# A new order of the matmuls, a later booking for one unit's values, and query loads joined into one

## The chip, the cores and the metric

The kernel runs on one core of a Trainium2 chip. The metric is the device time of one execution, in microseconds (us). A core has a matrix engine (TensorE, PE in the profile, with its weight loads as PEld), VectorE (DVE), ScalarE (ACT), GpSimd (POOL) and SyncE (SP), which in this kernel issues all DMAs.

## The reference

Two branches work on the same input `x` of 2048 rows of 512, and a gate per row mixes them. Branch A is attention with 32 heads of 16 columns that share one key and one value head; branch B is a gated feed-forward layer with 1792 inner columns. All is float32.

```python
q = (x @ wq).reshape(B, S, 32, 16)           # 32 query heads
k, v = x @ wk, x @ wv                        # one head of 16 columns each
p = softmax(einsum("bhqd,bkd->bhqk", q, k) * 16 ** -0.5)
a = einsum("bhqk,bkd->bhqd", p, v).reshape(B, S, 512) @ wo
b = (sigmoid(x @ w_gate) * (x @ w_up)) @ w_down
g = sigmoid((x * gate_w).sum(-1, keepdims=True))
return g * a + (1 - g) * b
```

## The kernel before

**The work.** The 2048 rows fall into four blocks of 512, and the heads into eight groups of four: 32 units of attention. Float32 operands of the projections are split into a high and a low part, so that one product becomes three matmuls. For a unit, line L1136 multiplies queries with keys to find each row's maximum (a "max" matmul, whose bank VectorE reduces on L1138), and L1145 multiplies again, the other way round and with the maximum taken off (a "score" matmul, whose bank ScalarE turns into exponentials `p` on L1147). Line L1009 multiplies `p` with the values (a "values" step of eight matmuls over all 128 rows of the array, here called V). Line L1110 is the feed-forward layer and the output projection (a "fill" matmul). Max, score and fill matmuls use one half of the array's rows, 64, and two of them run side by side, one in each half.

**The order is written out by hand.** `ORDER` is a string with one character for each step of TensorE. A hexadecimal digit is a slot: its two upper bits tell what the upper half does and its two lower bits what the lower half does (0 nothing, 1 max, 2 score, 3 fill). `V` is a values step, `G` a group of the first projections (L854) or a turn of the values (L926), and `.` no instruction at all, only a planned wait. V and G use the whole array, slots its halves; a run of V is opened after a slot and closed by the next slot. `plan()` walks the string with a model of all engines (class `State`), in which a slot is 100 units long. The model decides which of the eight PSUM banks each matmul takes (the one that has been free longest, `take`), and where each instruction of the other engines and each DMA stands in its engine's queue. The engines then run these queues in order, each waiting for what it needs. No time of the model is enforced on the chip. A booking in the model only keeps a string from being accepted in which a step comes too early: a bank that DVE has read counts as free `FREE` units after the read, one that ACT has read `FREE_A` units after it.

**Runs of V.** All V of a run add into one bank, taken when the run opens (`issue_v`), and when the run closes ACT copies that bank out (`finish`, L1016); if the unit has earlier runs, POOL adds the copy to theirs (L1023). So the bank that a run opens on must have been read out, by DVE if its last user was a max matmul (L1136), by ACT if it was a score matmul (L1145).

**Queries.** `store_q` writes the high and low part of a projected block of queries to DRAM (L955). `load_q` fetches a unit's queries into one of three tiles `qs` (L969): for each half of the array high, high and low part, 16 rows each, six DMAs of 64 KB; from the fourth unit on two DMAs of zeros follow (L971). The model books a load as six issues, in the changed kernel too. Unit u+1 is loaded when the max matmuls of unit u begin; the first two units are loaded together at the start.

**The end of a unit.** `store` sends the unit's sums and outputs to DRAM; `sums` fetches the sums (L1037) and the outputs `vd` (L1039); DVE inverts the sums (`invert`); `send_inverse` writes them back (L1047); `spread` fetches them spread over rows (`bc`, L1053); POOL multiplies the two (`divide`, L1058). Two units share a tile of 128 rows. Unit 30, the last but one (`NU - 2`), fills both halves of its own, so its fetches come twice; its result feeds the last fill matmuls (the `e` jobs). Unit 31 is finished in the tail, after the last V.

**Second halves of a fill job.** A fill job's two halves swap banks in the middle, and a marker on SP's queue (L1114) hands over: if SP is held up, that fill waits.

Of the kernel before, what the change touches and what calls it, by code (L numbers as in the profile page):

```python
# [9 lines left out]
F32 = mybir.dt.float32  # L10
# [7 lines left out]
S, D, H, DH, F = 2048, 512, 32, 16, 1792  # L18
# [34 lines left out]
IN, OUT, VALUES = 52, 106, 371  # L53
# [69 lines left out]
class State:  # L123
# [170 lines left out]
    def event(self, what, args):  # L294
# [374 lines left out]
    "GGGGGGG555G55G555G55......5G55GG555G55G555GG55G555GG5dddGff7f77ffffd757d.GG7fffdfffd7f7ffffdedee7edef7ef7b7b7b7b"  # L669
    "bdfedebdfbdb79ffef55VVVV7b76bfdbf9fbdef9fe7ededee7f6f7bdef6fdff7775VVV9deedef7edf9fbe77bfb7bb7bdff9edb7fedfd75dV"  # L670
    "VVVVGV6fede.edfef7efbb7f9fb7b7b7bfed9fbdb7fedbfed7d5VV655VVV7b7bb7fededbf9e7fbdededeef77b7ef9faf7d7f7ddVVVV5bb77"
    "bbbffde79fefededeede7bf77bfbd6fff7ddd5VVV566VV6ddefe7eedf6fbfe7b7b7b7bbdfbdfededbb7fedbf5VV555VVV97b7fbdbdbfb7eb"
    "fdedededeef76ffb76fef9f6fbf5V5a6V996VV696V559VVV7b7b7bbfdbdbedfe7edeeddee7fb7fed6feedf7777bVVVV9deeedf7fedb7bdef"
    "b7b7bb77eefddeedfef9b7ffdbddfedd5VVVVV6e9ff77bfb7b7bb77bfedbbdf6ff9f9ff.dd66VV659VV659VV7b7b7bbdfedbedfe79feedde"
    "e7f6f7bf9fbf6f6ffd5VVVVV7b97b7bbfdf9fee7efdedeede77efdbe7fee7feedfbdbfed9dVVVVV56fbfe7bfb7b7bb77bfbdafdbdf7bfedf"
    "de.56VV65aV6a5V955VVV97bbb77ffbdbdee7fededeede7f7b7bbfdbf9fbfb7e7aff775VVVV9dedfbdee7fedeeddef6fe7e7e7bfdbff775."
    "5VVVVV9deff9f6fbd6fedefb7b7b7bbdff9f9bf7ef97edefaV65eVVV959VV677bbfdfeeddee7f6ff797VVVdede7efb7b7b7bedbdff9eVVVd"
    "edede7ef6f6fbf97bfb7bb7bdff9f6efdbf6dbeff615.VVVVV6deededf7bf6feb7fbdb7bb7bbdfdfbdb7ef6edf5fdVVVVV5edeef7bfe7ede"
    "7e7bfb7b7bbdff9dbf6f9fedbf6fdV5a6V9aaVVVVV6dedef7ef6f6fbdbfb7e727b7bdef9fdbfbdef9f6f6f.9VV955VVV6edff6defb7ed6fb"
    "fe7b7bb7bdedfedfb7bf97edbfd4.9VV656VV5a5VV97bfdbdbe7f6fedefe7e763b7befdedefdbdefb7b79f.5VVV9a5V595VVV7b7afdedbf7"  # L680
    "b79fefbdedeedee77ff6f9fe7edb7bf7V95aV669V99aVV695VVV7b7afdf97efedef6fedb7b7bbdff96ffbd6fbffddd5VVVV677bbb7fdbfed"
    "bf6fededeede77fbfba7fdbf7fddd5VVVV767bbb7bffdedbe7fedededee7fb7f6ef7edbfd7f79VVVVV97bbb77fdef9f6fedefbde4ee7defe"
    "7dbf9fbb7f9ff55.VVVVVV7b79bffa7fdebdb7fededeedef7f6fe7e7bf9f9f6f7VVV969VV6edeedf7fb79fee7f9fb7b7bb7bfdedfbdef9f6"
    "ffd545.VVVVV96edffb7bf7edb7bbfdedeede7ef7defe7ebdb7bbf9VVVVV5baV9b7b7bb7fdfe7bedfedededee7ff6f67bfbdbfd7fd5VVVVV"
    "5edeeedfb7f6fe7bef7bb7b7bfddeefdbdbfa7f7eebV996V965VV5a9VV6a5VV6dedef7bfb79fbf9fb7edeede7ef7e7efdef97b7ffedefedd"
    "9VVVVV69f7bff6fb7b7bb7b7f9fedebdbf79ffefe5.6VV955VVV9b7b7fdbfb79fee7fededeede7ef7deef7ef67bffd9ffdedd5VVVVV67b7f"
    "bf9b7fe7b7bb7fededeedf7bbbd7ff5.5VVVVVdedede6ff6fb7bdb7efb7bb7bdef7edfedbf97bfed715.VV59aVVVV7b7bb5fee7fbdebdfbd"
# [564 lines left out]
```

## Time and profile before

| | us |
|---|---|
| median of 3 runs | 1583.15 |
| lowest and highest of them | 1582.33 and 1583.36 |
| the profiled execution | 1581.56 |
| its span, first to last instruction | 1579.8 |
| PE, DVE, ACT, POOL busy in it | 1570.6, 1335.6, 1223.0, 785.7 |

The profiled execution is 1.59 us faster than the median, and 1.76 us of its time lie outside the span. A busy engine is not an engine without waits: matmuls overlap, one record lasts 0.39 us while slots follow each other faster, so a wait shorter than the overlap leaves no idle time in PE's row. It is seen in the distance between the starts of two slots. The idle time of PEld, the weight loads, is not lost time by itself, since a weight load is short and runs beside the matmul before it.

### The profile page before, as it was taken

To read this page: it belongs to the slowest core of one execution; us is meant where nothing else is said; L and a number is where in the kernel's file an instruction comes from. 1 tells how busy PE (TensorE), PEld (TensorE's weight loads), DVE (VectorE), ACT (ScalarE), POOL (GpSimd) and SP (SyncE) were. 2 spreads that over 40 slices of the span, in tenths; PEclk is the share of its full clock that TensorE was granted. 3 is DMA by queue.
4 is the path that set the end of the run, shared out by engine and by line. 5 is a ranking of instruction groups with operands and counts; after the bars stand their busy time and mean duration, and the time that the engine had idled before them with its cause. 6 is when DMAs were issued, how large, how long until landed. Compare 5 with 4: busy or idle time off the path is not lost.

```text
span 1579.8 us, 33611 instructions
## 1 busy us (share of the span) xinstructions
PE 1570.6 (99%) x12910; PEld 1018.7 (64%) x12910; DVE 1335.6 (85%) x2280; ACT 1223.0 (77%) x2415; POOL 785.7 (50%) x713
## 2 busy tenths in 40 slices
PE   9999999999999999999999999999999999999998
PEld 7776766666666665756665666666666667676663
DVE  7998998988798888889889878897978899898852
ACT  4276778878788778868788877877878888787897
POOL 4226463745574164367466236265657426537351
PEclk9999999999999999999999999999999999999999
DMA  7413120212122121122121212022212212111011
GB/s 254 154 55 91 45 62 30 66 53 89 42 80 61 48 80 52 33 73 73 47 82 53 76 36 85 16 66 67 75 42 89 66 34 79 53 36 56 16 56 48
DMA packets 63077, 103.44 MB, mean 65 GB/s; under 512 B 24530, under 2 KB 24786, under 8 KB 62916
## 3 DMA queue, kind: packets, MB, share of 16 engines
q1 hardware_dynamic: 62916, 101.29, 20.5%
q8 instruction: 102, 1.67, 0.4%
q14 instruction: 59, 0.48, 0.1%
HBM read 79.51 MB, written 21.75 MB: 64 GB/s over the span
## 4 chain that ended last, share of the span: by engine, by line
PE 98%; DVE 1%; DMA 0%; POOL 0%; issue 0%; ACT 0%; DVEq 0%; SPq 0%; ACTq 0%
PE bank L1110 32%; PE bank L1009 29%; PE bank L1136 17%; PE bank L1145 16%; PE bank L854 3%; DVE mx L1138 1%; PE bank L1191 0%; DMA wkv_raw<-wkv 0%; POOL wkv_s L757 0%; PE bank L926 0%; DVE q L949 0%; DVE wkv_stack L890 0%; DVE ba L1200 0%; DVEq L1248 0%; ACT ou_last L1173 0%
## 5 line engine op out<-in xcount | busy, mean ns | idle before, releaser
L1138 DVE TENSOR_REDUCE mx<-bank 128x1 f32<-128x512 f32 x2048 | 1249.7, 680 | 172.9 <-PE bank L1136 85.9
L1147 ACT ACTIVATE p<-bank 128x512 f32<-128x512 f32 x2048 | 1037.2, 661 | 4.5 <-PE bank L1145 1.4
L1145 PE MATMUL bank<-qs,ks 64*128 64x512 f32 x2048 | 721.6, 401 | 0.0
L1136 PE MATMUL bank<-ks,qs 64*128 64x512 f32 x2048 | 680.7, 407 | 0.0
L1009 PE MATMUL bank<-p,v_aug 128*32 128x512 f32 x4096 | 477.5, 597 | 0.0
L1136 PEld LDWEIGHTS bank<-ks,qs 64*128 64x128 f32 x2048 | 337.5, 184 | 133.2 <-issue 49.7
L1145 PEld LDWEIGHTS bank<-qs,ks 64*128 64x128 f32 x2048 | 358.7, 184 | 89.5 <-ACT p L1147 20.1
L1016 ACT COPY ou<-bank 128x512 f32<-128x512 f32 x194 | 117.0, 603 | 281.1 <-PE bank L1009 196.0
L1023 POOL TENSOR_TENSOR ou<-ou,ou 128x512 f32<-128x512 f32 x163 | 210.0, 1288 | 210.9 <-ACT ou L1016 207.8
L1110 PE MATMUL bank<-wd,hl 64*128 64x512 f32 x1344 | 278.3, 391 | 0.1
L1110 PE MATMUL bank<-x,wu 64*128 64x512 f32 x1344 | 278.0, 391 | 0.1
L1009 PEld LDWEIGHTS bank<-p,v_aug 128*32 128x32 f32 x4096 | 114.7, 109 | 253.5 <-issue 208.5
L1110 PE MATMUL bank<-x,wg 64*128 64x512 f32 x1344 | 275.2, 391 | 0.0
L1110 PEld LDWEIGHTS bank<-wd,hl 64*128 64x128 f32 x1344 | 204.0, 184 | 19.7 <-issue 4.2
L1110 PEld LDWEIGHTS bank<-x,wu 64*128 64x128 f32 x1344 | 203.5, 185 | 14.8 <-issue 1.7
L1110 PEld LDWEIGHTS bank<-x,wg 64*128 64x128 f32 x1344 | 201.8, 185 | 16.1 <-issue 2.0
L1089 POOL TENSOR_TENSOR ba<-ba,pa_d 128x512 f32<-128x512 f32 x31 | 39.6, 1284 | 102.8 <-ACT pa_d L1086 102.8
L830 POOL CAST wg<-rg 128x1024 fp32r<-128x1024 f32 x27 | 28.0, 1038 | 123.5 <-PE bank L1110 66.2
L757 POOL TENSOR_TENSOR wd<-rd,wd 128x512 fp32r<-128x512 f32 x56 | 72.3, 1291 | 4.5
L757 POOL TENSOR_TENSOR hl<-h,hl 128x512 fp32r<-128x512 f32 x56 | 71.9, 1284 | 4.5
L1110 PE MATMUL bank<-wa,o 64*128 64x512 f32 x360 | 71.4, 393 | 0.0
L830 POOL CAST wu<-ru 128x1024 fp32r<-128x1024 f32 x27 | 28.0, 1038 | 82.1 <-PE bank L1110 65.0
(82 smaller groups left out, 745.1 us busy)
## 6 DMA issues: line engine op xcount, KB each, us to landing
rg<-wg SPq DMA_DIRECT2D x28, 512.0 KB
ru<-wu SPq DMA_DIRECT2D x28, 512.0 KB
rd<-wd SPq DMA_DIRECT2D x28, 512.0 KB
qs<-qd SPq DMA_DIRECT2D x192, 64.0 KB
qd<-q SPq DMA_DIRECT2D x32, 256.0 KB
od<-ou SPq DMA_DIRECT2D x31, 256.0 KB
xf<-x_in SPq DMA_DIRECT2D x16, 256.0 KB
vd<-od SPq DMA_DIRECT2D x32, 128.0 KB
```

Source lines behind the costliest of these rows:

```text
L757: lo.tensor_tensor(hl[:, 1, :], raw, f32(hl[:, 0, :]), op=ALU.subtract)
L830: nc.gpsimd.tensor_copy(WS[item][:, 0, :], raw)
L854: nc.tensor.matmul(ps, w[:, p, part(kc)], X[b, kc][:, q, :], start=i == 0, stop=i == 3 * KC - 1)
L1009: nc.tensor.matmul(ps[32 * j:32 * j + 32, :], v_aug[:, c, :], PT.pop((u, c, j)), start=start, stop=stop)
L1016: nc.scalar.copy(to, ps)
L1023: nc.gpsimd.tensor_tensor(SUMS[u], SUMS[u], PARTS_OF[u].pop(0), op=ALU.add)
L1089: nc.gpsimd.tensor_tensor(BA[b, t], BA[b, t], PA[b, t].pop(0), op=ALU.add)
L1110: ins = nc.tensor.matmul(banks[i], l, r, start=start, stop=stop)
L1136: nc.tensor.matmul(banks[i], qs_t[u % 3][r, pr, part(qt)], ks[r, kb * 512:(kb + 1) * 512], start=True, stop=True)
L1138: nc.vector.tensor_reduce(MX[u][:, pr, h, qt, kb:kb + 1], banks[i], axis=AX.X, op=ALU.max)
L1145: nc.tensor.matmul(banks[i], ks[r, part(c)], qs_t[u % 3][r, pr, :], start=True, stop=True)
L1147: nc.scalar.activation(p, banks[i], AF.Exp, scale=0.25)
```

## The change

The string `ORDER` is replaced. The new one has 4251 slots for 4263 (26 slots with an idle half become 2, and the matmuls stay the same), 512 V as before, in 197 runs for 182, 24 G in 12 groups for 11, and 19 planned waits for 43. The model's `FREE` goes from 30 to 65 units and `FREE_A` from 55 to 62, and some durations, in hundredths of a slot, are raised by about half a per cent.

`store_q` writes the high part twice, so that DRAM holds the three parts in the order of the tile, and `load_q` fetches a half with one DMA of 48 rows (192 KB) in the place of three. Its source has the parts as its outermost dimension. For unit 30 `sums` no longer fetches the outputs; `spread` does, each half behind that half's inverses, and `divide` is booked 2300 units later.

```diff
-LATE, LATE_A, FREE, FREE_A = 188, 196, 30, 55
+LATE, LATE_A, FREE, FREE_A = 188, 196, 65, 62
...
-RED, GATED, SUM, ENDS, INVERSE, LOWER = 258, 258, 285, 115, 70, 285
+RED, GATED, SUM, ENDS, INVERSE, LOWER = 260, 258, 285, 115, 70, 285
...
+SPREAD_TWICE = 2300
-EXP, COPY, SCALED = 208, 210, 247
+EXP, COPY, SCALED = 209, 211, 250
...
-IN, OUT, VALUES = 52, 106, 371
+IN, OUT, VALUES = 52, 109, 373
...
             if u % 2 or u == NU - 2:
-                self.task(2, at + 2 * SAFE, "divide", u)
+                self.task(2, at + 2 * SAFE + (u == NU - 2) * SPREAD_TWICE, "divide", u)
...
-    "GGGGGGG555G55G555G55......5G55GG555G55G555GG55G555GG5dddGff7f77ffffd757d.GG7fffdfffd7f7ffffdedee7edef7ef7b7b7b7b"
+    "GGGGG.GG555G55G555G55.......5G55GG555GG555GG7757G57fddfffffffdd..ddfffffffffd7775GG555GG555G55Ga7bfdfbdb7efbdb7f"
...
-        qd = dp.tile([2, 2, 2, DH, 2, TB], F32, name=f"qd{b}_{t}")
-        for i, half in enumerate(QD[b, t]):
+        qd = dp.tile([3, 2, 2, DH, 2, TB], F32, name=f"qd{b}_{t}")
+        for i, half in enumerate((QD[b, t][0], *QD[b, t])):
             nc.sync.dma_start(qd[i].rearrange("g par d pr t -> (g par d pr) t"), f32(half))
...
         for par in range(2):
-            for n, i in enumerate((0, 0, 1)):
-                r = 64 * par + n * DH
-                nc.sync.dma_start(qs[r:r + DH], qd[i, g % 2, par].rearrange("d pr t -> d (pr t)"))
+            r = 64 * par
+            nc.sync.dma_start(qs[r:r + 3 * DH], qd[:, g % 2, par].rearrange("n d pr t -> n d (pr t)"))
             if u > 2:
-                nc.sync.dma_start(qs[64 * par + 62:64 * par + 64], zeros)
+                nc.sync.dma_start(qs[r + 62:r + 64], zeros)
...
-        for r in (0, 64) if u == NU - 2 else (64 * (u % 2),):
+        if u == NU - 2:
+            VD["last"] = od
+        else:
+            r = 64 * (u % 2)
             nc.sync.dma_start(VD[u // 2][0][r:r + 64, :], od.rearrange("(j r) t -> j r t", j=4)[:, :DH, :])
...
         for r in (0, 64) if u == NU - 2 else (64 * (u % 2),):
             nc.sync.dma_start(VD[u // 2][1][r:r + 64, :], sums.unsqueeze(1).to_broadcast([4, DH, TB]))
+            if u == NU - 2:
+                nc.sync.dma_start(VD[u // 2][0][r:r + 64, :],
+                                  VD["last"].rearrange("(j r) t -> j r t", j=4)[:, :DH, :])
```

How the rows move on TensorE shows at the run of V that opens with step 2 of unit 5. A row has its line, the bank it writes, and its operands (`ks` keys, `qs` queries, `x`, `wu` and the like fill operands, `p` exponentials). Before, TensorE's queue there reads:

```order
L1145 MATMUL bank_79<-qs_109,ks 128x512
L1009 MATMUL bank_74<-p_1_0_0_4153,v_aug 32x512
L1009 MATMUL bank_74<-p_1_0_1_4071,v_aug 32x512
L1009 MATMUL bank_74<-p_1_1_0_4136,v_aug 32x512
L1009 MATMUL bank_74<-p_1_1_1_4064,v_aug 32x512
L1136 MATMUL bank_78<-ks,qs_107 128x512
L1145 MATMUL bank_72<-qs_109,ks 128x512
L1136 MATMUL bank_75<-ks,qs_108 128x512
L1136 MATMUL bank_73<-ks,qs_108 128x512
L1110 MATMUL bank_77<-x_1_125,wu_6_3965 128x512
L1145 MATMUL bank_76<-qs_109,ks 128x512
L1009 MATMUL bank_79<-p_2_0_0_4201,v_aug 32x512
```

The last row opens the run on bank_79, which a score matmul (L1145) wrote last, so an exponential on ACT has to have read it. In the changed kernel, whose max, score, fill and values lines are L1141, L1150, L1115 and L1008, TensorE's queue at the same step reads:

```order
L1141 MATMUL bank_76<-ks,qs_107 128x512
L1115 MATMUL bank_72<-x_1_125,wu_6_4002 128x512
L1115 MATMUL bank_75<-x_1_125,wu_6_4002 128x512
L1115 MATMUL bank_72<-x_1_125,wu_6_4002 128x512
L1141 MATMUL bank_78<-ks,qs_107 128x512
L1141 MATMUL bank_73<-ks,qs_107 128x512
L1115 MATMUL bank_75<-x_1_125,wu_6_4002 128x512
L1141 MATMUL bank_79<-ks,qs_107 128x512
L1115 MATMUL bank_75<-x_1_125,wu_6_4002 128x512
L1115 MATMUL bank_72<-x_1_125,wu_6_4002 128x512
L1141 MATMUL bank_74<-ks,qs_107 128x512
L1008 MATMUL bank_76<-p_2_0_0_4138,v_aug 32x512
```

The run now opens on bank_76, which a max matmul wrote and DVE has read. Counted over the whole queue, the runs of V before open 83 times on a bank last written by a max matmul, 66 times by a score matmul, 25 times by a fill and 8 times by an earlier V; in the changed kernel 144, 29, 17 and 7 times.

Of SP's DMAs at the start (`qd` the stored queries in DRAM, `qs` the units' query tiles, 107 for unit 0 and 108 for unit 1) its queue before holds:

```order
L955 DMA qd_0_204<-q_0_0_188 128x512
L955 DMA qd_0_204<-q_0_1_189 128x512
L955 DMA qd_1_236<-q_1_0_220 128x512
L955 DMA qd_1_236<-q_1_1_221 128x512
L969 DMA qs_107<-qd_0_204 16x1024 x6
L969 DMA qs_108<-qd_0_204 16x1024 x6
```

and in the changed kernel:

```order
L955 DMA qd_0_204<-q_0_0_188 128x512 x2
L955 DMA qd_0_204<-q_0_1_189 128x512
L955 DMA qd_1_237<-q_1_0_221 128x512 x2
L955 DMA qd_1_237<-q_1_1_222 128x512
L968 DMA qs_107<-qd_0_204 48x1x1024 x2
L968 DMA qs_108<-qd_0_204 48x1x1024 x2
```

The twelve loads of the first two units have become four, of three times the rows, and each store of a query block has a third DMA. Of SP's DMAs at unit 30 (`sd`, `od`, `rd` in DRAM) its queue before holds:

```order
L1031 DMA sd_20017<-ou_19455 4x512
L1032 DMA od_20018<-ou_19455 128x512
L1037 DMA rc_20066<-sd_20017 128x16
L1039 DMA vd_20015<-od_20018 64x1x512 x2
L1047 DMA rd_20109<-rc_20066 128x16
L1053 DMA bc_20016<-rd_20109 64x1x512 x2
```

and in the changed kernel:

```order
L1030 DMA sd_19940<-ou_19453 4x512
L1031 DMA od_19941<-ou_19453 128x512
L1036 DMA rc_19986<-sd_19940 128x16
L1049 DMA rd_20033<-rc_19986 128x16
L1055 DMA bc_19939<-rd_20033 64x1x512
L1057 DMA vd_19938<-od_19941 64x1x512
L1055 DMA bc_19939<-rd_20033 64x1x512
L1057 DMA vd_19938<-od_19941 64x1x512
```

The inverses no longer stand behind the two fetches of `vd`; these come between and behind the spread inverses.

More of the change, by code (lines that the diff above doesn't have):

```diff
@@ L674 @@
[L674 to L683, printed above, removed]
@@ new lines @@
+    "edeeded7bfe7be7def6ffb7f5.5VVVV9dedef7bfe7eb7defbdb7b7bbfde7fed9fb7fffdd55VVVV67b7bfdefe7bf9f6bfdededeef7f6efde7"
+    "efb7bb7f9VV555VVV9deededffb7bf67ee7f777bbbffedfedb7bdff7dd5VVVVV9b7efddefe76fedbfbdb7bb7b7fedbdf9fef6f6ff5dVVVVV"
+    "dedeeddefe7eb77bb7fb7b7bbfddefed6fbdef7f775VVVVdedededefb7b7be7bdfb7b7bbfddbbdfb7ef6edfef5VV955VVV977efbdbfe7bb7"
+    "f9fededdeee7fe77bfb7ede7eff79V955VVVVV7b7bb7b7fbdbededdefededeef7b7bf7edbfedbfbe6V555VVV7b7bb77bbfd6fedefededeed"
+    "dfbe7f6fedbbb7fdf75VV969V5a5VV569VV696V97bbfdbdfb7af7deef7edeede7f7edbfb7bf9f6ffd5VV565VVVdedaf7bf7ebdf6fedfb7b7"
@@ new lines @@
+    "bbdbdf9fef6f6fbdffd56VV565VVV5edeefdbf6fafd7bfbdb7bb7bfdf6efdedb7bbfdef5VV656VVV5ededeeff6fbe7bdfb7b7bb7bdfbdf9f"
+    "b7bdefedfe5V555VVVVV67bdfe7efedbed7efbdb7bb7bdfedfe7edee7bffb7aV955VVVV7b7bbddef9fb7e7bdefededee7fb7fedb7bde7eff"
+    "9bVVVVVV7b7b7bb7bdfeedf9fededeede7f7b7efb7efadfd77dVVVVV7b7bbfdedeededf6fbbfa7V95aV655VVdedeef7b7b7bb7fedbdf5dVV"
+    "7b7bb7f9fededee7fb7deeedef7f6bdfe7edbfbfb57VVVVV5edefee7fed9fe7bfb7b7bb7bfdedefd6febdbf7bf5VV956VVVde5edeeffe79f"
+    "eb7bf77bbb7bfdf9fedef97bf6ffd9V659VV695VVV97b7bf7bfedebd7bfededdeeef7f6fe7bdbb7ef7efaV955VVVVV5b7bfbdbf9f6fbedef"
@@ L713 @@
+    "aVV6edff6f9fbdef67b7fe9fbVVV6dfbf6bdfb7afdbdf6fbeeV5a9VVV7b7b7bb7fbdbdedefedededeef77b7bfb7bedfefeeaVVaaaVVVaaaV"
+    "VVeffbbffaffafaeVVbfbffbfbfeeeea8VVaaaVVaaaVVbfbefffbfbeeeeVbfeefefbffbbaVaaaVVVaaaVVeefbfffbaVV.....V"
 )
```

63 lines of the change are left out of this document (30 added, 33 removed).

## The prediction

> **What bounds the kernel now.** I read the page first, for busy shares and the chain of work that ended last, then TensorE's timeline for the distance between starts, then the list of waits, and last SP's timeline with the DMA table by stretches.
>
> ```profile
> PE 1570.6 (99%) x12910; PEld 1018.7 (64%) x12910; DVE 1335.6 (85%) x2280; ACT 1223.0 (77%) x2415; POOL 785.7 (50%) x713
> ...
> PE 98%; DVE 1%; DMA 0%; POOL 0%; issue 0%; ACT 0%; DVEq 0%; SPq 0%; ACTq 0%
> ```
>
> TensorE carries 98% of the chain. So the time is the number of its steps by what each costs, plus its waits, and other engines count only where TensorE waits for them. The price of a slot stands in its timeline (start, duration, engine, line):
>
> ```profile
> 600.04 0.39 PE L1145 MATMUL bank<-qs,ks 64*128 64x512 f32 x1
> ...
> 600.26 0.39 PE L1136 MATMUL bank<-ks,qs 64*128 64x512 f32 x1
> ...
> 600.50 0.39 PE L1145 MATMUL bank<-qs,ks 64*128 64x512 f32 x1
> ...
> 600.73 0.39 PE L1136 MATMUL bank<-ks,qs 64*128 64x512 f32 x1
> ...
> 601.42 0.42 PE L1145 MATMUL bank<-qs,ks 64*128 64x512 f32 x1
> ...
> 601.69 0.38 PE L1145 MATMUL bank<-qs,ks 64*128 64x512 f32 x1
> ```
>
> Three slots from 600.04 to 600.73 are 0.69 us, so a slot is 0.23 us. The pair at 601.42 is 0.27 apart: a wait of 0.04 that no idle time shows. Runs of V look so:
>
> ```profile
> 1541.56 0.40 PE L1145 MATMUL bank<-qs,ks 64*128 64x512 f32 x2
> 1541.90 1.92 PE L1009 MATMUL bank<-p,v_aug 128*32 128x512 f32 x16
> 1543.75 0.96 PE L1145 MATMUL bank<-qs,ks 64*128 64x512 f32 x6
> 1544.64 0.64 PE L1009 MATMUL bank<-p,v_aug 128*32 128x512 f32 x4
> ```
> ```profile
> 425.94 0.43 PE L1145 MATMUL bank<-qs,ks 64*128 64x512 f32 x1
> 426.05 0.39 PE L1136 MATMUL bank<-ks,qs 64*128 64x512 f32 x1
> 426.38 1.92 PE L1009 MATMUL bank<-p,v_aug 128*32 128x512 f32 x16
> ...
> 429.12 2.78 PE L1009 MATMUL bank<-p,v_aug 128*32 128x512 f32 x24
> 431.83 0.49 PE L1136 MATMUL bank<-ks,qs 64*128 64x512 f32 x1
> ```
>
> A run of two V lasts 1.85 us (1541.90 to 1543.75) and one of three 2.71 (429.12 to 431.83), so a V is 0.86. From opening to opening, 1541.90 to 1544.64, two V and three slots take 2.74; less 2 x 0.86 and 3 x 0.23 that leaves 0.33 for going into the whole array and out again. The opening itself is 0.34 after the last slot at 1541.56, but 0.44 at 425.94. The second one waits 0.10. Its bank was last written by a score matmul, nine matmuls earlier. Who ends such waits (waiter, releaser, total us, times, longest; PEld is the weight load in front of the matmul):
>
> ```profile
> PEld bank L1136 <- ACT p L1147: 23.8, 54, 0.8
> ...
> PEld bank L1136 <- DVE mx L1138: 22.7, 41, 0.8
> PEld bank L1009 <- ACT p L1147: 22.4, 71, 0.9
> PEld bank L1145 <- ACT p L1147: 20.1, 45, 0.8
> ...
> PEld bank L1145 <- DVE mx L1138: 14.9, 51, 0.8
> ...
> PEld bank L1009 <- DVE mx L1138: 10.8, 33, 0.4
> ```
>
> V's weight load (L1009) is released 71 times by an exponential and 33 times by a maximum, though more runs open on a bank from a max matmul (83) than from a score matmul (66). The totals are idle time of the loader, an upper bound on what TensorE lost.
>
> **The change, part by part.** *Slots.* Pairing the half-empty ones saves 12 slots by 0.23: -2.8 us.
>
> *Switches.* 15 more runs of V and one more group of G, 16 by 0.33: +5.3. Each new run also makes a copy and an addition:
>
> ```profile
> L1023 POOL TENSOR_TENSOR ou<-ou,ou 128x512 f32<-128x512 f32 x163 | 210.0, 1288 | 210.9 <-ACT ou L1016 207.8
> ...
> L1016 ACT COPY ou<-bank 128x512 f32<-128x512 f32 x194 | 117.0, 603 | 281.1 <-PE bank L1009 196.0
> ```
>
> 15 by 0.60 on ACT and by 1.29 on POOL lie in the 23% and 50% that these engines idle: nothing, at most 9 us if ACT were the bound.
>
> *Openings.* 37 fewer runs open on a bank that ACT has to free (66 to 29). At the 0.10 of the row at 425.94 this is -3.7. The ends are 0, if the bank isn't the cause, and -12.6, if all loader idle counted (22.4 by 37/66). I take the price nearest to the term, the one measured at an opening.
>
> *Slots' own waits.* `FREE` grows by 35 units, 0.08 us at 0.23 a slot, which exceeds the wait of 0.04 at 601.69. The two rows with DVE hold 92 waits; at 0.04 they are 3.7 us. `FREE_A` grows by 7 units, 0.02 us, so the 99 waits for ACT mostly stay. I take half of 3.7, -1.8, since fuller slots ask for banks more densely; the ends are 0 and -7.6 (all 191). The planned waits, 43 to 19, issue nothing and are not counted again.
>
> *SP's queue.* A unit's load drops from six issues to two, so markers of fill jobs wait less behind it:
>
> ```profile
> L1110 PEld LDWEIGHTS bank<-wd,hl 64*128 64x128 f32 x1344 | 204.0, 184 | 19.7 <-issue 4.2 <-ACT pa_d L1086 0.8 <-SPq L1114 0.8
> L1110 PEld LDWEIGHTS bank<-x,wu 64*128 64x128 f32 x1344 | 203.5, 185 | 14.8 <-issue 1.7 <-SPq L1114 0.4 <-DVE mx L1138 0.2
> ```
>
> TensorE lost at most 1.2 us to them; I take -0.5.
>
> *The joined load.* Its source has three parts as outermost dimension. The nearest rows are those of `vd` and `bc`, whose source has four. First SP, POOL and TensorE at unit 30, then two stretches with the share of the 16 DMA engines and GB/s at the end; in the first of them only the two `vd` loads run:
>
> ```profile
> 1552.01 1.07 SPq L1053 DMA_DIRECT2D bc<-rd  x2
> ...
> 1557.30 1.30 POOL L1058 TENSOR_TENSOR vd<-vd,bc 128x512 f32<-128x512 f32 x1 [16.50 <-DMA bc<-rd]
> ...
> 1564.70 0.50 PE L1110 MATMUL bank<-we,o 64*128 64x512 f32 x1
> ```
> ```profile
> 1546.50:1548.50 2.00, 2.00 (x22) 1.00 (x22) 0.00 (x0) 2.00 (x5) 0.00 (x0) 1.00 0.26 100
> ...
> 30.00:40.00 10.00, 9.90 (x47) 6.64 (x45) 9.64 (x17) 5.46 (x11) 7.30 (x6) 1.00 1.04 369
> ```
>
> A share of 0.26 is four engines, 25 GB/s each, where other transfers reach 369 on sixteen. So I estimate three engines and 75 GB/s for the new load: 192 KB in 2.6 us, both halves in 5.2. Two `bc` of 128 KB took 5.29 us from issue to POOL, 2.6 of it for the bytes, so some 2.7 come on top. Later a load is issued when the max matmuls of the unit before begin, up to a unit's time ahead (1579.8 / 32 = 49 us), which hides 8 us; if that cover were gone, each of 30 loads would cost up to 8. At the start there is no such cover:
>
> ```profile
> 18.21 6.39 SPq L969 DMA_DIRECT2D qs<-qd  x12
> ...
> 20.61 3.02 PE L854 MATMUL bank<-x,wkv_s 128*128 128x512 f32 x12
> 23.56 1.30 PE L1136 MATMUL bank<-ks,qs 64*128 64x512 f32 x6
> ```
>
> The first max matmul runs at 23.56 without a gap. With both halves there at 18.21 + 5.2 + 2.7 = 26.1 it would wait 2.5. I take +2.0, as part of the 2.7 is the second issue, which overlaps. The ends are 0 (the twelve small loads were in time) and +7.7, below. The third store of each block is issued while SP waits for the next block.
>
> *Unit 30.* Its divide began at 1557.30 and its fills only at 1564.70, so nothing waits. The inverses lose the two `vd` loads in front of them, and these come behind instead: the divide starts about when it did. Zero; the cover is some 4 us after the divide's own 3.4.
>
> The sum is -2.8 + 5.3 - 3.7 - 1.8 - 0.5 + 2.0 = -1.5 us. Against the profiled execution, 1581.56, this is 1580.1; the median of the runs lies 1.6 higher, so 1581.6.
>
> **The rivals.** *The margins clear most waits.* Openings -6 (the fill banks too, and longer waits than 0.10), slots -5, the start +1.0: -2.8 + 5.3 - 6 - 5 - 0.5 + 1 = -8.0, 1575.1. For it speaks that the loader's waits add up to over 100 us; against it, that the one slot wait I can price is 0.04.
>
> *An opening costs what it costs.* If the wait comes from draining the halves before the whole array is used, the bank doesn't matter, the openings' term is 0 and the sum +2.2, 1585.4. Against it: openings at 1541.90 and 426.38 follow the same kind of slot and differ by 0.10. The Trainium skill, "TensorEngine Tiling (Array Packing)", section Tiling Modes, states such a drain at every change of tiling mode.
>
> *The joined load costs nothing.* If it spreads over sixteen engines after all, it lands before 23.56, as two issues take less of SP than six: the sum without the +2.0 is -3.5, 1579.6. Against it: the stretch at 1546.50, where a load with an outermost four moves 100 GB/s. The Trainium skill, "DMA: Bandwidth & Descriptors", section Bandwidth, says to batch DMAs, and that transfers under 64 KB are dominated by descriptors; by that page the joined load can only gain.
>
> *The first loads are served in turns* (slower). If three engines serve the loads of units 0 and 1 side by side, unit 0 is complete only with all four: 18.21 + 10.4 + 2.7 = 31.3, a wait of 7.7 in the place of 2.0. The sum is +4.2, 1587.4. It decides from a wait of 6.7 on. Against it: the small loads of one queue were issued, and used, one after another.
>
> **How the numbers follow.** The forecast has a chance of 0.32, the cleared waits 0.28, the free load 0.10, the fixed opening cost 0.12, the loads in turns 0.18. A measurement tells about 0.2%, 3.2 us, from no change. The forecast and the fixed opening lie within it: 0.44 same; the cleared waits and the free load 0.38 faster; the loads in turns 0.18 slower. The range goes from 1574.5, just below the cleared waits, to 1588, just above the loads in turns.
>
> **What would show it.** TensorE's first max matmul at some 25.5 us in place of 23.56 with a DMA as releaser; fewer waits of L1008's weight load ended by ACT, about 30 for 71; fewer slot waits ended by DVE; the same 0.33 at a clean switch; and the fills of unit 30 without a wait. The forecast is wrong if the new order waits for something that the old one never met, such as POOL behind a weight load that is itself queued behind a three-engine query load.

## The result and the profile after

| | before | after |
|---|---|---|
| median, us | 1582.91 (6 runs, 1581.33 to 1583.82) | 1587.76 (6 runs, 1587.41 to 1591.08) |
| profiled execution, us | 1581.56 | 1591.08 |
| its span, us | 1579.8 | 1589.3 |

The changed kernel is slower: the ratio is 1.0036, with a 95% interval of 1.0025 to 1.0046, and the medians lie 4.85 us apart. The profiled execution of the changed kernel lies 3.3 us above its median; some 2.1 of that is a slow first stretch, shown at the end.

The page's first line and the chain of work that ended last, after:

```profile
PE 1572.6 (99%) x12910; PEld 1016.0 (64%) x12910; DVE 1340.6 (84%) x2279; ACT 1230.4 (77%) x2429; POOL 804.5 (51%) x727
...
PE 96%; DMA 1%; DVE 1%; ACT 0%; POOL 0%; issue 0%; SPq 0%; DVEq 0%; POOLq 0%; ACTq 0%
PE bank L1115 32%; PE bank L1008 29%; PE bank L1141 16%; PE bank L1150 16%; PE bank L854 2%; DMA qs<-qd 1%; DMA md<-sq 1%; DVE mx L1143 0%; POOL wg L831 0%; DVE q L949 0%; DMA qs<-md 0%; ACT x L781 0%; PE bank L1196 0%; DMA wkv_raw<-wkv 0%;
```

TensorE carries 96% of the chain in place of 98%, and two transfers have come onto it: the query load, and `md`, by which the maxima are put into place for the scores. In order of time the chain has them here (start, us, what):

```profile
21.27 8.87 DMA qs<-qd
31.83 4.32 PE bank L854 x12
...
84.36 8.45 DMA md<-sq
```

And TensorE's timeline at both places:

```profile
23.73 2.00 PE L854 MATMUL bank<-x,wkv_s 128*128 128x512 f32 x8
26.47 0.50 PE L1141 MATMUL bank<-ks,qs 64*128 64x512 f32 x1 [0.74 <-DMA qs<-qd]
30.18 1.65 PE L1141 MATMUL bank<-ks,qs 64*128 64x512 f32 x5 [3.22 <-DMA qs<-qd]
31.76 4.39 PE L854 MATMUL bank<-x,wq 128*128 128x512 f32 x12
...
95.13 0.47 PE L1150 MATMUL bank<-qs,ks 64*128 64x512 f32 x1 [3.18 <-DMA qs<-md]
```

The first max matmul waits 0.74 us for the first half of unit 0's queries, the second 3.22 us for the other half, and the first score matmul 3.18 us for the maxima. The twelve query matmuls at 31.76 take 4.3 us; twelve like them took 3.0 us before. The reason stands in the column of the granted clock. The same execution by stretches (stretch, length, busy time of PE, PEld, DVE, ACT and POOL, granted clock, DMA share, GB/s):

```profile
29.00:30.00 1.00, 0.00 (x0) 0.00 (x0) 0.00 (x0) 0.00 (x0) 0.00 (x0) 0.50 0.22 74
30.00:35.00 5.00, 4.82 (x13) 3.45 (x14) 3.08 (x5) 0.00 (x0) 0.00 (x0) 0.53 0.46 146
96.00:99.00 3.00, 3.00 (x16) 2.75 (x18) 1.38 (x2) 1.56 (x4) 0.00 (x0) 0.52 1.03 384
```

From 28 to 35 us, and from 96 to 99, TensorE has half its clock: each wait is followed by a stretch of slow work. The first row has every other engine idle and a DMA share of 0.22 at 74 GB/s, near the 0.19 of three engines in sixteen; by this share the joined load runs on three. The Trainium skill, "DMA: Bandwidth & Descriptors", section Rules for kernel authors, says that an outermost dimension of fewer than 16 confines a DMA to at most that many engines; the source here has 3, and the trace agrees.

SP's timeline, and below it who ended SP's waits between 20 and 40 us:

```profile
20.38 3.02 SPq L968 DMA_DIRECT2D qs<-qd  x4
...
25.09 12.47 SPq L766 DMA_DIRECT2D xf<-x_in  x8
...
80.53 1.47 SPq L968 DMA_DIRECT2D qs<-qd  x2
...
84.36 0.40 SPq L993 DMA_DIRECT2D md<-sq  x1
...
92.86 1.39 SPq L1001 DMA_DIRECT2D qs<-md  x2
```
```profile
SPq L766 <- DMA qs<-qd: 9.1, 4, 3.4
```

Before, SP's timeline had:

```profile
25.59 3.81 SPq L766 DMA_DIRECT2D xf<-x_in  x8
```

SP took 12.47 us to issue eight loads of the next rows of `x`, where it had taken 3.81: for 9.1 us it was held until a joined load was done.

Elsewhere the new order did what was forecast. Who ended the waits of TensorE's loader, after:

```profile
PEld bank L1150 <- ACT p L1152: 36.5, 76, 0.8
PEld bank L1141 <- ACT p L1152: 33.0, 65, 0.8
PEld bank L1008 <- ACT p L1152: 10.8, 31, 0.6
PEld bank L1141 <- DVE mx L1143: 10.3, 17, 0.8
PEld bank L1008 <- DVE mx L1143: 8.9, 29, 0.4
...
PEld bank L1150 <- DVE mx L1143: 2.8, 5, 0.8
```

V's waits ended by an exponential fell from 71 to 31, and the slots' waits ended by a maximum from 92 to 22 (17 and 5). The slots' waits ended by an exponential rose from 99 to 141 (76 and 65). Averaged over all openings, the distance from the last slot's first matmul to the first V fell from 0.380 us to 0.359; what that distance holds is taken up under the openings.

### The profile page after: what moved, and what is told of

Same layout as the page of the kernel before. It is cut to its first block, busy times and chain, and to the rows that moved or that the text cites. A ratio compares the mean times of both kernels' runs of the same rounds, so it can differ in the third digit from the quotient of the medians.

```text
span 1589.3 us, 33458 instructions
## 1 busy us (share of the span) xinstructions
PE 1572.6 (99%) x12910; PEld 1016.0 (64%) x12910; DVE 1340.6 (84%) x2279; ACT 1230.4 (77%) x2429; POOL 804.5 (51%) x727
## 4 chain that ended last, share of the span: by engine, by line
PE 96%; DMA 1%; DVE 1%; ACT 0%; POOL 0%; issue 0%; SPq 0%; DVEq 0%; POOLq 0%; ACTq 0%
PE bank L1115 32%; PE bank L1008 29%; PE bank L1141 16%; PE bank L1150 16%; PE bank L854 2%; DMA qs<-qd 1%; DMA md<-sq 1%; DVE mx L1143 0%; POOL wg L831 0%; DVE q L949 0%; DMA qs<-md 0%; ACT x L781 0%; PE bank L1196 0%; DMA wkv_raw<-wkv 0%; DVE x L787 0%
## 5 line engine op out<-in xcount | busy, mean ns | idle before, releaser
L1150 PE MATMUL bank<-qs,ks 64*128 64x512 f32 x2048 | 726.0, 399 | 3.5 <-DMA qs<-md 3.5
L1141 PE MATMUL bank<-ks,qs 64*128 64x512 f32 x2048 | 678.0, 406 | 4.0 <-DMA qs<-qd 4.0
L1008 PE MATMUL bank<-p,v_aug 128*32 128x512 f32 x4096 | 480.9, 597 | 0.0
L1150 PEld LDWEIGHTS bank<-qs,ks 64*128 64x128 f32 x2048 | 360.0, 184 | 104.9 <-ACT p L1152 36.5
L1141 PEld LDWEIGHTS bank<-ks,qs 64*128 64x128 f32 x2048 | 337.8, 184 | 133.9 <-issue 50.6
L1015 ACT COPY ou<-bank 128x512 f32<-128x512 f32 x207 | 127.8, 617 | 277.9 <-PE bank L1008 133.4
L1022 POOL TENSOR_TENSOR ou<-ou,ou 128x512 f32<-128x512 f32 x176 | 227.0, 1290 | 175.4 <-ACT ou L1015 171.7
L1115 PE MATMUL bank<-x,wu 64*128 64x512 f32 x1344 | 274.2, 392 | 0.1
L1115 PE MATMUL bank<-wd,hl 64*128 64x512 f32 x1344 | 273.2, 390 | 0.0
L1115 PE MATMUL bank<-x,wg 64*128 64x512 f32 x1344 | 271.8, 391 | 0.0
L1008 PEld LDWEIGHTS bank<-p,v_aug 128*32 128x32 f32 x4096 | 113.2, 109 | 247.3 <-issue 219.4
L1115 PEld LDWEIGHTS bank<-x,wu 64*128 64x128 f32 x1344 | 204.4, 185 | 18.0 <-issue 2.5
L1115 PEld LDWEIGHTS bank<-wd,hl 64*128 64x128 f32 x1344 | 203.8, 184 | 17.2 <-issue 3.4
L1115 PEld LDWEIGHTS bank<-x,wg 64*128 64x128 f32 x1344 | 201.1, 184 | 16.9 <-issue 2.5
L1115 PE MATMUL bank<-wa,o 64*128 64x512 f32 x360 | 69.9, 391 | 0.2 <-SPq L1119 0.2
```

Of the source, the lines that this page charges most:

```text
L1008: nc.tensor.matmul(ps[32 * j:32 * j + 32, :], v_aug[:, c, :], PT.pop((u, c, j)), start=start, stop=stop)
L1015: nc.scalar.copy(to, ps)
L1022: nc.gpsimd.tensor_tensor(SUMS[u], SUMS[u], PARTS_OF[u].pop(0), op=ALU.add)
L1115: ins = nc.tensor.matmul(banks[i], l, r, start=start, stop=stop)
L1141: nc.tensor.matmul(banks[i], qs_t[u % 3][r, pr, part(qt)], ks[r, kb * 512:(kb + 1) * 512], start=True, stop=True)
L1150: nc.tensor.matmul(banks[i], ks[r, part(c)], qs_t[u % 3][r, pr, :], start=True, stop=True)
```

## The experiments

My theory was that the loss is the three-engine load with what follows from it, and that the order gains about what was forecast. The rival was that the new order itself starts badly. Medians in the table are in us; each ratio is to runs of the kernel before on the same chip.

| kernel | median | ratio, 95% interval |
|---|---|---|
| six loads, new order | 1578.92 | 0.9972 (0.9961 to 0.9982) |
| wide load, new order | 1576.95 | 0.9963 (0.9951 to 0.9976) |
| units 0 and 1 in small loads, new order | 1579.93 | 0.9984 (0.9974 to 0.9993) |
| joined load, old order | 1591.37 | 1.0055 (1.0041 to 1.0068) |
| wide load, old order | 1580.91 | 0.9992 (0.9982 to 1.0001) |
| wide load, margins back at 30 and 55 | 1576.47 | 0.9962 (0.9948 to 0.9976) |
| wide load, `FREE_A` at 0 | 1579.08 | 0.9979 (0.9970 to 0.9989) |
| wide load, old unit 30 | 1576.93 | 0.9965 (0.9952 to 0.9978) |
| wide load, old order, `FREE` at 0 | 1583.38 | 1.0007 (0.9997 to 1.0016) |
| after, unit 1 in small loads | 1589.08 | 1.0038 (1.0025 to 1.0051) |
| after, 32 useless matmuls in the wait | 1590.49 | 1.0050 (1.0035 to 1.0065) |
| after, 12 useless matmuls in the wait | 1585.40 | 1.0019 (1.0009 to 1.0030) |

### The old loads under the new order

```diff
-        qd = dp.tile([3, 2, 2, DH, 2, TB], F32, name=f"qd{b}_{t}")
-        for i, half in enumerate((QD[b, t][0], *QD[b, t])):
+        qd = dp.tile([2, 2, 2, DH, 2, TB], F32, name=f"qd{b}_{t}")
+        for i, half in enumerate(QD[b, t]):
...
-            nc.sync.dma_start(qs[r:r + 3 * DH], qd[:, g % 2, par].rearrange("n d pr t -> n d (pr t)"))
+            for n, i in enumerate((0, 0, 1)):
+                r = 64 * par + n * DH
+                nc.sync.dma_start(qs[r:r + DH], qd[i, g % 2, par].rearrange("d pr t -> d (pr t)"))
```

> The changed kernel with the queries stored and loaded as before (high part stored once, six loads of 16 rows a unit); order, margins and unit 30 stay changed. Theory 'narrow loads': the loss is the two waits of TensorE for query transfers (4.0 and 3.5 us in the changed kernel's profile) and the half clock behind each (some 2.3 and 1.5 us), 11.3 us in an execution of 1591.1. Both go, the clock stays at 1.00, and the time is 1578 to 1581. Rival 'the new order starts badly whatever the loads are': 1586 to 1588, with the same two waits.

It took 1578.92 us, 8.8 below the changed kernel, inside the theory's range. No wait of TensorE for a DMA is left. So the joined load and its third store cost 8.8 us, and the rest of the change gains 3.8 (1578.92 against 1582.71). Seven runs of six loads fall into two groups, as is told with the wide load; against the lower one, at 1577.1, the cost is 10.7.

### The joined load under the old order

The same edit the other way round: the kernel before gets the change's `store_q` and `load_q`.

```diff
-        for i, half in enumerate(QD[b, t]):
+        for i, half in enumerate((QD[b, t][0], *QD[b, t])):
...
-            for n, i in enumerate((0, 0, 1)):
-                r = 64 * par + n * DH
-                nc.sync.dma_start(qs[r:r + DH], qd[i, g % 2, par].rearrange("d pr t -> d (pr t)"))
+            r = 64 * par
+            nc.sync.dma_start(qs[r:r + 3 * DH], qd[:, g % 2, par].rearrange("n d pr t -> n d (pr t)"))
```

> The kernel before with only the joined load and the third store of the change; old order, old margins, old unit 30. Theory 'narrow loads': the first max matmul, without a gap before, waits some 4 us, and the half clock behind it costs 2 to 4 more; 1587 to 1592. Rival 'the new order starts badly': 1582 to 1584.

1591.37, 8.7 us more than the kernel before: near the same price without the new order, though it is made up in another way. TensorE's timeline shows the first wait and the slow matmuls behind it, and SP's waits are the same 9.1 us:

```profile
25.00 0.50 PE L1135 MATMUL bank<-ks,qs 64*128 64x512 f32 x1 [0.98 <-DMA qs<-qd]
28.64 1.65 PE L1135 MATMUL bank<-ks,qs 64*128 64x512 f32 x5 [3.15 <-DMA qs<-qd]
30.22 4.59 PE L854 MATMUL bank<-x,wq 128*128 128x512 f32 x12
```
```profile
SPq L766 <- DMA qs<-qd: 9.1, 4, 3.3
```

The second wait, for the maxima, is not there. Step against step of the kernel before, this execution is 7.3 us behind at 98 us, and it loses 3.0 more between 586 and 595 us, where a unit's two narrow loads stand ahead of a load of weights, `rd`. SP, POOL, DVE and TensorE there:

```profile
570.34 0.73 SPq L968 DMA_DIRECT2D qs<-qd  x1
...
571.59 0.41 SPq L749 DMA_DIRECT2D rd<-wd  x1
...
580.80 0.61 POOL L756 CAST wd<-rd 128x512 fp32r<-128x512 f32 x1 [4.85 <-DMA rd<-wd]
...
588.62 0.21 DVE L989 STREAM_TRANSPOSE sq<-ms 128x32 f32<-128x32 f32 x1 [3.12 <-POOL ms L983]
...
589.46 0.49 PE L1144 MATMUL bank<-qs,ks 64*128 64x512 f32 x1 [1.38 <-DVE mx L1137]
```

The weights are used 9.2 us after their issue, where the kernel before used them after 4.1 (565.28 to 569.34). POOL comes late to the split of the maxima, DVE waits for that, the reductions behind it free their banks late, and TensorE waits 1.38 us, and 1.12 more for a marker of a fill at 594.66. It is the kind of chain that the prediction named last, weights queued behind a three-engine load, met in the old order. The trace shows it; no run tests it by itself.

The rival, that the new order starts badly, falls with these two runs.

### The joined load made wide

The columns of the query weights are permuted where the inputs are laid out, so that the 16 columns of a head lie outermost in a stored part. A load's source is then 48 rows at one even distance.

```diff
-        qd = dp.tile([3, 2, 2, DH, 2, TB], F32, name=f"qd{b}_{t}")
+        qd = dp.tile([3, DH, 2, 2, 2, TB], F32, name=f"qd{b}_{t}")
...
-            nc.sync.dma_start(qd[i].rearrange("g par d pr t -> (g par d pr) t"), f32(half))
+            nc.sync.dma_start(qd[i].rearrange("d g par pr t -> (d g par pr) t"), f32(half))
...
-            nc.sync.dma_start(qs[r:r + 3 * DH], qd[:, g % 2, par].rearrange("n d pr t -> n d (pr t)"))
+            nc.sync.dma_start(qs[r:r + 3 * DH], qd[:, :, g % 2, par].rearrange("n d pr t -> (n d) (pr t)"))
...
-    wq = np.asarray(A_wq).reshape(D, NT, 2, 2, 2, DH).transpose(0, 1, 2, 4, 5, 3)
+    wq = np.asarray(A_wq).reshape(D, NT, 2, 2, 2, DH).transpose(0, 1, 5, 2, 4, 3)
```

> The changed kernel with the joined load kept, but the columns of the query weights in another order, so that a stored part has its rows outermost and the load's source is 48 evenly spaced rows in place of 3 parts of 16. Theory 'narrow loads': it is the outermost three that keeps a load on three DMA engines; now the load takes sixteen, both waits go, and the time is that of six loads or up to 1 us less, 1577 to 1581. Rival 'a joined load is late in any shape, since the third store stands ahead of it': a wait of 2 us or more at the first max matmul, 1584 to 1588.

1576.95 us, 10.8 below the changed kernel, with as many DMAs and bytes as that has. TensorE reaches the first max matmul and the first score without a gap, and SP gives out the eight `x` loads in 4.58 us:

```profile
23.55 1.19 PE L1141 MATMUL bank<-ks,qs 64*128 64x512 f32 x6
24.67 3.06 PE L854 MATMUL bank<-x,wq 128*128 128x512 f32 x12
...
83.44 0.50 PE L1150 MATMUL bank<-qs,ks 64*128 64x512 f32 x2
```
```profile
23.20 4.58 SPq L766 DMA_DIRECT2D xf<-x_in  x8
...
71.84 1.23 SPq L968 DMA_DIRECT2D qs<-qd  x2
...
75.90 0.43 SPq L993 DMA_DIRECT2D md<-sq  x1
...
79.50 1.49 SPq L1001 DMA_DIRECT2D qs<-md  x2
```

This kernel beats both the one before and the one after. Whether it also beats six loads is open: 1.97 us lie between the medians, but runs of the six loads fall into two groups (1576.8 to 1577.3 and 1578.9 to 1579.9), and the lower one lies where this kernel does.

With the wide load under the old order (against the joined load under it):

```diff
-            nc.sync.dma_start(qs[r:r + 3 * DH], qd[:, g % 2, par].rearrange("n d pr t -> n d (pr t)"))
+            nc.sync.dma_start(qs[r:r + 3 * DH], qd[:, :, g % 2, par].rearrange("n d pr t -> (n d) (pr t)"))
```

> The kernel before (old order, old margins, old unit 30) with the joined load in its wide form and the third store. Theory 'the order gains, the load costs nothing once it is wide': 1581 to 1583, no wait at the first max matmul, against 1582.7 for the kernel before. Rival 'part of the gain of the wide kernel comes from the fewer issues': 1578 to 1580.

1580.91, a ratio of 0.9992 with 1 inside its interval. A wide load under the old order costs nothing and gains nothing that can be told.

### Which loads cause which wait

Here only units 0 and 1 go back to six small loads each; the third store stays.

```diff
+            if u < 2:
+                for n in range(3):
+                    nc.sync.dma_start(qs[r + n * DH:r + (n + 1) * DH], qd[n, g % 2, par].rearrange("d pr t -> d (pr t)"))
+            else:
```

> The changed kernel with only units 0 and 1 loaded in six small loads each (from the three stored parts); all later units keep the joined load. If the second wait (for the maxima of unit 0) comes only from SP being held up at the start, both waits go: 1578 to 1581. If it comes from unit 2's joined load and the third stores ahead of the maxima on SP's queue, the first goes and the second stays: 1582 to 1585. Rival 'the new order starts badly': 1586 to 1588.

1579.93. The first wait is gone, and of the second 1.5 us are left; so the loads of two units out of 32 caused 7.8 of the 8.8 us. The rest of the second wait belongs to unit 2's narrow load, as TensorE's and SP's timelines show:

```profile
86.51 0.47 PE L1154 MATMUL bank<-qs,ks 64*128 64x512 f32 x1 [1.22 <-DMA qs<-md]
```
```profile
73.20 1.61 SPq L972 DMA_DIRECT2D qs<-qd  x2
...
77.71 0.41 SPq L997 DMA_DIRECT2D md<-sq  x1
...
84.23 1.40 SPq L1005 DMA_DIRECT2D qs<-md  x2
```

From the issue of `md` to the next step, which waits for it, 6.5 us pass here, 3.6 with the wide load, 1.9 with six loads and 8.5 in the changed kernel. A small transfer behind a narrow load is late, though it is not narrow itself. What makes the 8.5 out of 6.5 was not separated; the stretch before it also carries the transfers that SP gave out late.

### In turns or in order

One of the prediction's rivals had unit 0 late because unit 1's loads share its engines. Here unit 1 alone is loaded in small pieces.

```diff
-            if u < 2:
+            if u == 1:
```

> The changed kernel with unit 1 alone loaded in six small loads; unit 0 and all others keep the joined load. In the changed kernel the two halves of unit 0 were there 6.1 and 9.8 us after the first of the four loads was issued. Theory 'served in turns' (unit 0 is late because unit 1's loads share its three engines): the second half comes 1 to 2 us behind the first, TensorE waits under 2.5 us, and the time is 1581 to 1585. Rival 'served in order' (unit 0's loads are slow by themselves): the second half again some 3.7 us behind the first, 4 us of waiting, 1586 to 1588.

1589.08, 1 us above the second theory's range. TensorE's timeline, and the issue of unit 0's loads:

```profile
25.55 0.50 PE L1145 MATMUL bank<-ks,qs 64*128 64x512 f32 x1 [1.81 <-DMA qs<-qd]
28.05 1.65 PE L1145 MATMUL bank<-ks,qs 64*128 64x512 f32 x5 [2.00 <-DMA qs<-qd]
```
```profile
18.41 1.61 SPq L972 DMA_DIRECT2D qs<-qd  x2
```

The second half is used 9.6 us after the first issue, as in the changed kernel (20.38 to 30.18, 9.8). The gap between the halves fell to 2.5 us, but because the first half came later. Unit 0's loads are as slow without unit 1's narrow ones beside them, and the rival falls, although its forecast time, 1587.4, lies within 0.4 of the measured one.

### The half clock

To price it, useless matmuls fill the wait between the first and the second max matmul. They write a bank that the second then overwrites.

```diff
+        if s == pr == 0 and h == 1:
+            for _ in range(32):
+                nc.tensor.matmul(banks[i][:, :P], ident, ident, start=True, stop=True)
```

> The changed kernel with 32 small matmuls of no use (the identity with itself, 128 columns, some 0.09 us each) between TensorE's first and second max matmul, where it waits 3.2 us for the second half of unit 0. Theory 'idle time halves the clock': the granted clock stays at 1.00 behind that wait, the twelve query matmuls behind it take 3.0 us in place of 4.3, and the time falls by 1 to 3 us, to 1585 to 1587; the second wait and its half clock stay. Rival 'the clock falls for another reason': 0.50 again behind the wait, and 1587.5 to 1589.

1590.49, outside the expected range: the 32 matmuls took 7.4 us, 0.23 each and not 0.09, and became the wait themselves. But the clock stayed at 1.00 there, and the query matmuls took 3.0 us. It did fall later, at 95.30 us, behind the second wait, which was only 1.36 us long in this run:

```profile
93.56 1.05 PE L1153 MATMUL bank<-qs,ks 64*128 64x512 f32 x2 [1.36 <-DVE q L949]
```

So I sized them again, with 12:

```diff
-            for _ in range(32):
+            for _ in range(12):
```

> As the kernel with 32 small matmuls of no use between the first two max matmuls, but with 12 of them: the 32 took 7.4 us, 0.23 each, and held up the second max matmul themselves; 12 take 2.8 us, less than the wait of 3.2 us that they fill. Theory 'idle time halves the clock': the clock stays at 1.00 until the second wait, the twelve query matmuls take 3.0 us, and the time is 1 to 2 us below the changed kernel's 1587.8, 1585.5 to 1586.8. Rival 'the half clock cost nothing that is not given back later, at the second wait': 1587.3 to 1588.3.

1585.40 us, 2.4 below the changed kernel. TensorE's timeline and a stretch of the profiled execution:

```profile
24.96 0.50 PE L1144 MATMUL bank<-ks,qs 64*128 64x512 f32 x1 [1.20 <-DMA qs<-qd]
25.39 2.94 PE L1143 MATMUL bank<-consts 128*128 128x128 f32 x24
29.20 0.97 PE L1144 MATMUL bank<-ks,qs 64*128 64x512 f32 x5 [0.86 <-DMA qs<-qd]
30.10 3.06 PE L854 MATMUL bank<-x,wq 128*128 128x512 f32 x12
```
```profile
30.00:35.00 5.00, 5.00 (x22) 3.52 (x22) 3.95 (x7) 0.59 (x1) 0.00 (x0) 1.00 0.44 154
```

Busy time that does nothing made the kernel faster: the idle time itself is what halves the clock. This one stands on medians 2.4 us apart, and its eight runs spread over 4.4 us, so the size is rough. Nor is it the price of the first half clock alone. Step against step of the changed kernel, and without the slow first stretch of that, the profiled execution gains 1.0 us up to the end of the twelve query matmuls and 3.2 around the second wait, which lasts 1.79 us here in place of 3.18 and has no half clock behind it. Why that wait is shorter was not separated.

### Why openings became cheaper

The prediction put an opening's wait down to the kind of bank, the ones that ACT has to free. The margins test that: with the order fixed they only choose which bank each matmul takes.

```diff
-LATE, LATE_A, FREE, FREE_A = 188, 196, 65, 62
+LATE, LATE_A, FREE, FREE_A = 188, 196, 30, 55
```

> The wide kernel with its order unchanged, but the model's margins back at 30 and 55 units. The margins now only choose which bank each matmul takes: 81 runs of V open on a bank that a score matmul wrote last (29 in the wide kernel) and 91 on one that a max matmul wrote (144). Theory 'an opening waits for ACT's bank', 0.06 to 0.10 us for each of the 52: 3 to 5 us more, 1580 to 1582, and the mean distance from the last slot to an opening rises by 15 to 26 ns. Rival 'an opening costs what it costs': 1576.5 to 1577.5.

1576.47, no slower. With 81 openings on banks of score matmuls in place of 29 the mean distance to an opening is 0.356 us, against 0.357. The theory of the kind of bank falls here.

The other direction:

```diff
-LATE, LATE_A, FREE, FREE_A = 188, 196, 65, 62
+LATE, LATE_A, FREE, FREE_A = 188, 196, 65, 0
```

> The wide kernel with its order unchanged and FREE_A at 0 in place of 62, so that only 12 runs of V open on a bank that a score matmul wrote last (29 in the wide kernel). Theory 'an opening waits for ACT's bank', 0.06 to 0.10 us for each of the 17: 1 to 1.7 us less, 1575.2 to 1576. Rival 'the wait moves into the slots, which now take banks that ACT has only just read': 1577 to 1580, with more waits of max and score weight loads ended by ACT.

1579.08: the rival was right. The openings gain 1.6 ns each, but the slots now take banks that ACT has just read. Their waits ended by an exponential are 183, against 137 with the wide load:

```profile
PEld bank L1150 <- ACT p L1152: 41.9, 104, 0.8
PEld bank L1141 <- ACT p L1152: 36.5, 79, 0.8
```

Summed over all slots the distances grow by 2.3 us. The profiled execution also has the slow first stretch, 1.9 us up to its first query matmul.

Last, more openings on ACT's banks under the old order, with the wide load:

```diff
-LATE, LATE_A, FREE, FREE_A = 188, 196, 30, 55
+LATE, LATE_A, FREE, FREE_A = 188, 196, 0, 55
```

> The kernel before with the wide load (old order), and FREE at 0 in place of 30, which moves bank choices alone: 92 runs of V open on a bank that a score matmul wrote last (66), 57 on one from a max matmul (83). Theory 'the kind of bank costs', 0.06 us for each of the 26: 1.5 us more, 1582 to 1583, with the mean distance to an opening up by 8 ns from 378. Rival 'only the time since the bank was read counts': 1580.3 to 1581.5 and a mean distance within 3 ns of 378.

1583.38, 2.5 more than the wide load under the old order, and the mean distance to an opening rose from 0.378 to 0.385 us, which is 1.2 us over the openings. The time is 0.4 above the theory's range, and the 7 ns are near its 8. Here the kind of bank does show: those on a score matmul's bank cost 0.407 us, those on a max matmul's 0.345. So under the old order the kind goes with the cost, and under the new one it does not. The distance in matmuls since the bank was written explains a part: under the old order it is 12 on the mean for score banks and 14 for max banks, and with the new order and the old margins it is 14 for both, which both cost 0.36. But in the wide kernel with the new margins the 29 on score banks, at 12.5, cost 0.337, less than the 144 on max banks at 14.1, which cost 0.361. That it is not the choice of banks alone is shown.

Much of the difference lies ahead of the opening, since the distance is taken from the first of the last slot's two matmuls. The prediction's rows show that the two can start together (1541.56) or 0.11 us apart (425.94 and 426.05). Taken from the later one, the mean is 0.341 us before and 0.333 with the wide load. In the kernel before, 16 openings come within two slots of a half-empty slot and cost 0.468 from the first matmul; 13 of them are on a score matmul's bank, and the new order has one such opening left. Without them, and from the later matmul, openings on score and on max banks cost 0.335 and 0.332: there the kind does not count. It does with `FREE` at 0, where the same two are 0.353 and 0.326. What the slots ahead of a run wait for under the old order stays open.

### Unit 30

The wide kernel with the outputs of unit 30 fetched by `sums` again:

```diff
-        if u == NU - 2:
-            VD["last"] = od
-        else:
-            r = 64 * (u % 2)
+        for r in (0, 64) if u == NU - 2 else (64 * (u % 2),):
             nc.sync.dma_start(VD[u // 2][0][r:r + 64, :], od.rearrange("(j r) t -> j r t", j=4)[:, :DH, :])
...
-            if u == NU - 2:
-                nc.sync.dma_start(VD[u // 2][0][r:r + 64, :],
-                                  VD["last"].rearrange("(j r) t -> j r t", j=4)[:, :DH, :])
```

> The wide kernel with unit 30's outputs fetched as before the change, by the step that fetches the sums. Theory 'unit 30 costs nothing either way': 1576.5 to 1577.5. Rival 'the late fetch holds back the last fills': 1574 to 1576.

1576.93, against 1576.95. That part of the change costs nothing.

## Why the prediction was wrong

The forecast was 1581.6 and no change; measured were 1587.76 and slower, at the upper edge of the range.

**The joined load** is the step that failed. It stood in the sum at +2.0, with ends of 0 and +7.7, and it cost 8.8 us in the new order and 8.7 in the old. Three engines and 74 GB/s were right, and so was the place of the first wait. It was priced as one wait alone, and three things were left out or mis-sized:

- The wait at the first max matmuls was worked out as 2.5 and cut to 2.0; TensorE idled 4.0 us. The second half was used 9.8 us after the first issue, and I had counted 7.9. From 25 to 28 us, while it was on its way, loads of `x` and stores kept all sixteen engines busy (shares of 0.92 to 1.05); that they held it up is likely, but not shown.
- The half clock behind a wait was no term at all. Step against step of the profiled execution with six loads, it costs 2.1 us behind the first wait (1.4 in the twelve query matmuls, the rest in the slots ahead of them) and 1.7 behind the second. The Trainium skill, "TensorE: Matmul & The Clock Gate", section What's actually happening, states half the rate after an idle window of some 3.4 us. The traces agree on the half and on steps of 3.41 us, but not on the idle: TensorE was busy for 1.75 us of the 3.41 ahead of the first fall, and for 1.93 of those ahead of the fall behind the wait of 1.36 us.
- "Up to a unit's time ahead, which hides 8 us" was true of the loads and not of what stands behind them. SP was held for 9.1 us, `md` came late behind unit 2's load, and the scores of unit 0 waited 3.5 us. In the old order it was weights that came late, for 3.0 us.

Together 4.0 + 2.1 + 3.5 + 1.7 are 11.3 us in the profiled execution of 1591.08. The span of the one with six loads, whose first stretch was as slow, is 12.4 us shorter, so some 1.1 us are not accounted for.

**Slots and switches** (-2.8 and +5.3): the steps are as many as forecast. The strings have 13 groups of G for 14, one of the 14 between two V, and the runs between slots are 16 more all the same. What the pairing saved was not measured by itself: a half-empty slot took 0.12 us to the next and not 0.23, and cost time behind it, as the 16 openings at 0.468 show. A run of V with its closing, taken from the mean distances of the trace, costs 0.34 over its V and slots, against the 0.33 used, and that includes what is left of the waits.

**Openings** (-3.7): 197 openings at 0.357 us against 0.380 are -4.5 in the wide kernel, near the term, but that is luck. The reason was wrong, since giving 52 of them back to ACT's banks changed nothing. And the price was misread: the row at 425.94 shows no wait of 0.10 for a bank. The slot's second matmul starts at 426.05 and V 0.33 us behind it, no later than at 1541.56, where both start together; the 0.10 is the distance between the slot's halves. From the later matmul the openings are worth -1.5 (0.333 against 0.341), which lies nearer to the 0 of the rival "an opening costs what it costs" than to -3.7.

**The slots' own waits** (-1.8, ends 0 and -7.6): summed over all slots, the distances fell by 3.5 us with the wide load and by 1.1 in the changed kernel, leaving out its waits for transfers but not the half clock. The waits for DVE went as forecast (92 to 22); those for ACT, which were to stay, grew from 99 to 141.

**SP's queue** (-0.5): zero. TensorE's waits for the markers of fill jobs total 1.2 us after, as before; there was nothing to gain.

**Unit 30** (0): right, with less cover than I named. The divide began at 1570.31, counted from the end of the span 3.5 us later than before, and its fills at 1573.95, 0.3 us after POOL's last part of the split.

Without the load the terms sum to -3.5; six loads measured -3.8 and the wide load -5.8, so the near hit is partly chance, with the openings misread and the slots' waits too small. Of the rivals, "the joined load costs nothing" is what the wide load made true; that a joined load can only gain, as the prediction read the advice to batch, failed with 8.8 us. And "loads in turns" came near in time by a mechanism that the runs deny.

## What to carry to other kernels

Joining small transfers pays only if the joined one still spreads over the DMA engines: look at the outermost dimension of both sides, and lay the data out for it. Price a late transfer by its wait, by the slow clock behind the wait, and by what stands behind it in the issuing queue and on the same engines, not by the transfer alone. When a cost and a property go together in one order, change the property alone before taking it for the cause.

## What the runs showed of the hardware

- SP does not run ahead without limit: while four narrow loads were under way, its next eight issues took 12.47 us in place of 3.81, and the trace names the narrow loads as what released them. A load of weights behind two narrow loads was used 9.2 us after its issue, in place of 4.1.
- The granted clock changed in steps of 3.41 us. The trace of the changed kernel has it at 0.50 from 27.88 to 34.70 us and from 96.14 to 99.56; it came back 4.5 us after work had resumed at 30.18. Within the first 100 us the traces have six such falls, each behind a step in which TensorE was busy for 0.67 to 1.93 us, and none behind a step with 2.20 or more. So the length of one wait does not decide: one of 1.36 us brought the clock down (32 useless matmuls), and one of 1.79 did not (12 of them). Busy time alone is no full rule either: within the last 10 us of four runs the clock stayed whole behind steps with 1.40 to 1.58 us.
- The first projection has two paces. TensorE's timeline of the changed kernel, and then of the wide one:

```profile
8.03 3.60 PE L854 MATMUL bank<-x,wkv_s 128*128 128x512 f32 x9
```
```profile
7.19 2.33 PE L854 MATMUL bank<-x,wkv_s 128*128 128x512 f32 x9
```

The same nine matmuls take 3.6 or 2.3 us, and all that follows is 2.1 us later or not. The profiled executions of six loads and of the units 0 and 1 in small loads had the slow pace too, those of the kernel before and of the joined load under the old order the fast one. So it does not follow the order or the loads. The views give a clock of 1.00 in both, but they count a stretch without a record as whole: the clock record begins at 10.81 us in the changed kernel and at 4.83 in the wide one, at 10.49 to 10.81 in all five slow profiled executions and at 4.19 to 6.55 in the nine fast ones. In the changed kernel TensorE ran four of these matmuls in a microsecond up to 11 us, and six behind. That the clock is at half until then is likely, but not recorded. It fits the two groups in the runs of one kernel, but only profiled executions show it, and what sets the moment stays open.
